# Cached attention and a gated MLP for one token: from groups of four heads with two K and two V buffers to groups of eight heads with three shared buffers

## The chip, the cores and the metric

The kernel runs on one core of a Trainium2 chip. Its work is done by five engines that run side by side and meet at semaphores: TensorE (PE; its weight loads are listed apart, as PEld), VectorE (DVE), ScalarE (ACT), GpSimd (POOL) and SyncE (SP), which issues nearly all transfers from HBM. PE multiplies what lies in SBUF and writes to PSUM. The metric is the device time of one execution in microseconds, lower is better; three executions of the kernel before were timed.

## What is computed

One token passes through an attention block with a long cache and then through a gated MLP, with a layer norm ahead of each and a residual after each. Everything is bf16; D = 640, 32 heads of 128, 4096 cached positions, MLP width 1728.

```
h = x + attention(layernorm(x)) @ wo
    q      = layernorm(x) @ wq                      # 32 heads x 128
    scores = q . k_cache * 128**-0.5                # 32 x 4096
    o      = softmax(scores) @ v_cache              # 32 x 128
h2 = h + (gelu(g) * u) @ w_down                     # g, u = layernorm(h) @ w_gate, w_up
```

K and V are 33.6 MB each, wq and wo 5.2 MB each, the three MLP matrices 2.2 MB each: 84.23 MB, each byte of which is used once.

## The kernel before, in words

`Sched` keeps a list of operations per engine, in the order in which the Python code calls them, and for each the semaphores it waits for. So the order of calls is the order of each engine's queue, and an engine whose first instruction waits holds back all behind it. SP's queue, which issues the loads, is such a queue too.

Heads are worked on in 8 groups of 4 (`HG`, `NG`). For a group, K is laid out with 32 partitions a head and 128 positions on each (`R`), 32 KB a partition, 4 MB in all; V likewise. There are two buffers for K and two for V, three product buffers `prod`, two score buffers `sc` and two probability buffers `P4`. The weights wq and wo share the `arena`; w_gate, w_up and w_down reuse K and V buffers when the last groups are done with them.

- Query (`query`, L318, L324): PE multiplies wq with x broadcast over 128 columns, five matmuls a group, and ACT copies each head's row onto its partitions in `qb`. It is done one group ahead.
- Scores, in four pieces of 32 positions: DVE multiplies K by q into `prod` (`mult`, L339), PE sums groups of 16 elements with an identity matrix (`fold`, eight matmuls, L359 and L350), and DVE sums the last 16 (`red`, L366).
- Softmax: a maximum on DVE, turned by PE (L378), a maximum over each head's partitions (L383), broadcast by PE (L388), and four exps on ACT, one per head, which write `P4` and the row sums (L395).
- Values (`values`, L406): matmuls with 16 columns of P as weights and 512 columns of V, all to the same 16 partitions of PSUM. `extract` (L421, L424) takes the useful blocks on DVE, `column` (L429) turns them. For the last group `values_last` (L414) uses V as weights.
- w_o (`project`, L612): the attention result is re-laid out (`spread`, `gather`, `place`) per pair of groups and multiplied with wo as weights, 160 matmuls of 32 columns, of which three quarters are issued ahead of the last group's values.
- Layer norm (L282 to L297), MLP (`up`, L659: 70 matmuls for gate and 70 for up, weights as the stationary side), gelu by an exp (L666 to L675), and the down projection (L697: 60 matmuls of 160 columns with one column of h as weights, to partitions 0, 32, 64 and 96). The last 64 rows of w_down come by eight small loads and a gathered vector (`rest`).

The loop over groups is written out as a software pipeline. In step n, DVE multiplies group n and finishes the maximum of group n-1, PE folds group n and between the folds runs the values of groups n-1 and n-2 in quarters. K(n+2) is issued once group n's products are made, V(n) once the values of group n-2 are done:

```python
        t_mul[3] = kfree[n] = mult(n, 3)
        if beside:
            values(p, 0, CH)
        fold(n, 3, t_mul[3])
...
            if n >= 2:
                load_v(n)
            if n + 2 < NG:
                load_k(n + 2)
```

Of the kernel before, what the change touches and what calls it, by code (L numbers as in the profile page):

```python
# [11 lines left out]
D = 640  # L12
H = 32
# [9 lines left out]
HG = 4  # L23
# [5 lines left out]
VR = 4  # L29
VM = VR * HG  # L30
NW = 4
HW = H // NW
DJ = 128 // HW
NFT = 13
NF = NFT + 1
WD_PARTS = (5, 4, 3, 1)

WD_COLS = []
for _n in WD_PARTS:
    _b = 128 * len(WD_COLS)  # L40
    WD_COLS += [(_b, _n, _i) for _i in range(_n)]
FREM = DF - NFT * 128
NRR = 2
NRP = FREM // NRR // 2
NRK = 32 + NRP
WIDE = 32
# [67 lines left out]
def bass_sequential_preLN__gqa_block_cached__glu_gated_geglu__decode_kernel(  # L114
# [16 lines left out]

    arena = sb("arena", [128, NC_D * H * DH], BF16)
    kbuf = [sb("kbuf%d" % i, [128, R, DH], BF16) for i in range(2)]
    vbuf = [sb("vbuf%d" % i, [128, R, DH], BF16) for i in range(2)]

    def over(name, base, shape):
        return nc.alloc_sbuf_tensor_at(name, shape, BF16, offset=nc.lookup_mloc(base).addr)

    wq_sb = over("wq_sb", arena, [128, NC_D, H * DH])
    wo_sb = over("wo_sb", arena, [128, NW, HW, D])
    wg_sb = over("wg_sb", kbuf[NG % 2], [128, NC_D, DF])
    wu_sb = over("wu_sb", kbuf[(NG + 1) % 2], [128, NC_D, DF])
    wd_sb = over("wd_sb", vbuf[NG % 2], [128, NFT + NRR, D])

    NPR = 3
    prod = [sb("prod%d" % i, [128, RP, DH], BF16) for i in range(NPR)]
    qb = sb("qb", [128, NG, DH], BF16)
    sc = [sb("sc%d" % i, [128, R], FP32) for i in range(2)]  # L150
    P4 = [sb("P4_%d" % i, [128, R, HG], BF16) for i in range(2)]
    RS = sb("RS", [128, H], FP32)
    mx = sb("mx", [128, NG], FP32)
    mrow = sb("mrow", [1, H], FP32)
    nb = sb("nb", [128, H], FP32)
    rz = sb("rz", [128, H], FP32)
    xm = sb("xm", [VM, VR, DH], FP32)
    xz = [sb("xz%d" % i, [VM, DH], FP32) for i in range(2)]
    rmask = sb("rmask", [VM, VR], FP32)
    hsel = sb("hsel", [VM, HG], FP32)  # L160
    aT = sb("aT", [128, H], BF16)
    aL = sb("aL", [128, HW, DJ], BF16)
    aP = sb("aP", [128, H], BF16)
    jmask = sb("jmask", [128, DJ], BF16)
    csel = sb("csel", [128, HW], BF16)
    jred = sb("jred", [128, DJ], FP32)
    cred = sb("cred", [128, HW], FP32)
# [8 lines left out]
    g_t = sb("g_t", [128, NF], FP32)  # L176
    t1 = sb("t1", [128, NF], FP32)
    t2 = sb("t2", [128, NF], FP32)
    t3 = sb("t3", [128, NF], FP32)
    e_t = sb("e_t", [128, NF], FP32)  # L180
    d_t = sb("d_t", [128, NF], FP32)
    r_t = sb("r_t", [128, NF], FP32)
    gu = sb("gu", [128, NF], FP32)
    hm = sb("hm", [128, NF], BF16)
    hq = sb("hq", [128, NRR], BF16)
    hr = sb("hr", [128, NRR], BF16)
    hcol = sb("hcol", [128, NRR], FP32)
    hrow = sb("hrow", [128, 128], BF16)
    o_sb = sb("o_sb", [128, D // 4], BF16)
    hx = sb("hx", [128, 32, NC_D], FP32)  # L190
    m32 = sb("m32", [128, 32], FP32)
    e4 = sb("e4", [128, 4], FP32)
# [3 lines left out]
    ones_bf = sb("ones_bf", [128, 128], BF16)  # L196
# [3 lines left out]
    pq = nc.alloc_psum_tensor("pq", [128, 512], FP32)  # L200
    pm = nc.alloc_psum_tensor("pm", [128, 512], FP32)
    po = nc.alloc_psum_tensor("po", [128, 512], FP32)
    pz = nc.alloc_psum_tensor("pz", [128, 512], FP32)
    pg = nc.alloc_psum_tensor("pg", [128, 512], FP32)
    pu = nc.alloc_psum_tensor("pu", [128, 512], FP32)
    pv = [pg, pu]


    t_one = S.op("vector", lambda v: v.memset(ones[:, :], 1.0))
    t_part = S.op("vector", lambda v: v.memset(part[:, :], 1.0 / D))  # L210
    S.op("vector", lambda v: v.memset(eps[:, :], EPS))
    t_onebf = S.op("vector", lambda v: v.memset(ones_bf[:, :], 1.0))
    t_p4 = [S.op("vector", lambda v, i=i: v.memset(P4[i][:, :, :], 0.0)) for i in range(2)]
    t_rs = S.op("vector", lambda v: v.memset(RS[:, :], 0.0))
# [3 lines left out]
    t_ibf = S.op("gpsimd", lambda g: g.affine_select(  # L218
        Ibf[:, :], ones_bf[:, :], pattern=[[1, 128]], compare_op=ALU.is_equal,
        fill=0.0, base=0, channel_multiplier=-1), [t_onebf])  # L220

    t_e4 = S.op("vector", lambda v: v.reduce_sum(
        e4[:, :], I32[:, :].rearrange("p (j i) -> p j i", j=4), axis=AX.X), [t_i32])
    hsum = hx[:, :, :].rearrange("p a b -> p (a b)")[:, 0:2 * NRP]
    t_hsum = S.op("vector", lambda v: v.reduce_sum(
        hsum, I32[:, 128 - FREM:128].rearrange("p (r i) -> p r i", i=NRR), axis=AX.X))
    t_hrow = S.op("vector", lambda v: v.memset(hrow[:, :], 0.0))
    t_hrow = S.op("vector", lambda v: v.tensor_copy(
        hrow[:, 0:64].rearrange("p (b r) -> p b r", b=2)[:, :, 0:NRP],
        hsum.rearrange("p (b r) -> p b r", b=2)), [t_hsum, t_hrow])  # L230
    t_hcol = S.op("vector", lambda v: v.reduce_sum(
        hcol[:, :], I32[:, 128 - FREM:128].rearrange("p (r i) -> p i r", i=NRR), axis=AX.X))
    t_m32 = S.op("vector", lambda v: v.reduce_sum(
        m32[:, :], I32[:, :].rearrange("p (j i) -> p i j", j=4), axis=AX.X))
    S.op("vector", lambda v: v.reduce_sum(
        rmask[:, :], I32[0:VM, 0:VM].rearrange("p (j h) -> p j h", h=HG), axis=AX.X))
    t_hsel = S.op("vector", lambda v: v.reduce_sum(
        hsel[:, :], I32[0:VM, 0:VM].rearrange("p (j h) -> p h j", h=HG), axis=AX.X))
    a = S.op("vector", lambda v: v.reduce_sum(
        jred[:, :], I32[:, :].rearrange("p (j c) -> p j c", c=HW), axis=AX.X))  # L240
    b = S.op("vector", lambda v: v.reduce_sum(
        cred[:, :], I32[:, :].rearrange("p (j c) -> p c j", c=HW), axis=AX.X))
    t_jm = S.op("vector", lambda v: v.tensor_copy(jmask[:, :], jred[:, :]), [a])
    t_cs = S.op("vector", lambda v: v.tensor_copy(csel[:, :], cred[:, :]), [b])


    d_wq = S.dma("sync", "wq", lambda s: s.dma_start(  # L247
        wq_sb[:, :, :], A_wq[:, :].rearrange("(p c) n -> p c n", c=NC_D)))

    def cache(src, g):  # L250
        return src[0, g * HG:(g + 1) * HG, :, :].rearrange("h (q r) d -> (h q) r d", r=R)

    d_k, d_v = [None] * NG, [None] * NG
    kfree, vfree = [None] * NG, [None] * NG

    def load_k(g):
        d_k[g] = S.dma("sync", "k%d" % (g % 2), lambda s: s.dma_start(
            kbuf[g % 2][:, :, :], cache(A_k_cache, g)), [kfree[g - 2] if g >= 2 else None])


    def load_v(g):
        d_v[g] = []
        cuts = [0, R]
        for i in range(len(cuts) - 1):
            lo, hi = cuts[i], cuts[i + 1]
            tok = S.dma("sync", "v%d_%d" % (g % 2, i), lambda s, lo=lo, hi=hi: s.dma_start(
                vbuf[g % 2][:, lo:hi, :], cache(A_v_cache, g)[:, lo:hi, :]),
                [vfree[g - 2] if g >= 2 else None])
            d_v[g] += [tok] * (hi - lo)


    load_k(0)
    load_k(1)
    load_v(0)


# [4 lines left out]
    def layernorm(src, t_src, o, dst, ps, beside=None):  # L281
        b = S.op("vector", lambda v: v.scalar_tensor_tensor(  # L282
# [4 lines left out]
        if beside is not None:  # L287
            beside()
        q = 2 * o
        d = S.op("vector", lambda v: v.scalar_tensor_tensor(  # L290
# [6 lines left out]
        return S.op("vector", lambda v: v.tensor_scalar(  # L297
# [3 lines left out]
    for c in range(NC_D):  # L301
        a = S.op("tensor", lambda t, c=c: t.matmul(
            pm[:, c:c + 1], x_sb[0:1, c::NC_D], ones_bf[0:1, 0:1],
            start=(c == 0), stop=(c == NC_D - 1), skip_group_check=True),
            [d_x, t_onebf], token=(c == NC_D - 1))
    t_x32 = S.op("vector", lambda v: v.tensor_copy(x32[:, :], pm[:, 0:NC_D]), [a])
    t_x32 = S.op("vector", lambda v: v.reduce_sum(st[:, 0:1], x32[:, :], axis=AX.X), [t_x32])
    t_xb = layernorm(x32, t_x32, 0, (
        xb[:, :, :], x32[:, :].unsqueeze(2).to_broadcast([128, NC_D, 128])), pz)


    t_qb = [None] * NG

    def query(g):
        tok = None
        for c in range(NC_D):
            n0 = g * HG * DH
            tok = S.op("tensor", lambda t, c=c, n0=n0: t.matmul(  # L318
                pq[:, :], xb[:, c, :], wq_sb[:, c, n0:n0 + HG * DH],
                start=(c == 0), stop=(c == NC_D - 1)),  # L320
                [t_xb, d_wq, t_qb[g - 1] if g else None], token=(c == NC_D - 1))
        for hh in range(HG):
            lo, hi = hh * PPH, (hh + 1) * PPH
            t_qb[g] = S.op("scalar", lambda a, lo=lo, hi=hi, hh=hh: a.copy(  # L324
                qb[lo:hi, g, :], pq[lo:hi, hh * DH:(hh + 1) * DH]), [tok])
        return tok


    fold_done, red_done = {}, {}
    t_exp, t_pv = [None] * NG, [None] * NG  # L330
    t_ext, t_acc = [None] * NG, [None] * NG
# [404 lines left out]
```

## Time and profile before

| | |
|---|---|
| device time, median of 3 | 203.99 us (203.86 to 205.19) |
| device time of the profiled execution | 203.82 us |
| its span in the profile | 202.6 us |
| granted TensorE clock, mean | 0.935 |
| bytes read from HBM | 84.23 MB, 416 GB/s over the span |

The span is the profiled part of an execution, from its first instruction to its last; the device time has 1.2 us more around it. The profile gives busy time by engine, 40 equal slices of the span, the transfer queues, the chain that ended last (followed back from the last instruction, at each step to what released it), and groups of instructions by line: their busy time in all, the mean length of one in ns, and the idle time of the engine just ahead of them with what ended it. Matmuls are pipelined, so a matmul's length is not the distance to the next; that distance is read from the timeline. Loads take these times from issue to landing, queueing included: K 25.1 us and V 23.2 us (medians), wq 15.3, w_gate 22.6, w_up 27.3.

### The profile page before, as it was taken

The numbers are of one execution on the slowest core, as the hardware profiler recorded it, in microseconds if no ns is written. First come the engines' busy times: TensorE is split into PE (matmuls) and PEld (weight loads), VectorE is DVE, ScalarE is ACT, GpSimd is POOL, SyncE is SP. The second block draws the span as 40 slices with busy tenths as digits, with TensorE's granted clock in tenths as the row PEclk, the third lists the DMA queues.
The fourth block names the chain that finished last, engine by engine and source line by source line (L and its number), as shares of the span: only waits on it lengthen the run. The fifth ranks groups of instructions, "written<-read, shape, count | busy, mean of one in ns | idle before, by whom it ended". The sixth has DMA issues, their size and how long they took to land.

```text
span 202.6 us, 2291 instructions
## 1 busy us (share of the span) xinstructions
PE 153.4 (76%) x1084; PEld 49.8 (25%) x860; DVE 116.1 (57%) x153; ACT 30.5 (15%) x110; POOL 2.4 (1%) x8
## 2 busy tenths in 40 slices
PE   1005348689969957999899399959777999977775
PEld 1001000002211220322122113212100244666572
DVE  6200087998199518883993499269999513301121
ACT  2002200006004200150060006000604004000000
POOL 1000000000000000000000000000000000200000
PEclk9999999999999996999999999999999999975555
DMA  7999999999999999999999999999999999989992
GB/s 251 412 469 414 414 434 453 459 414 414 421 450 427 459 409 414 440 429 440 443 421 414 434 440 440 434 427 411 440 427 446 385 427 457 450 382 438 423 396 102
DMA packets 3939, 84.37 MB, mean 416 GB/s; under 512 B 441, under 2 KB 570, under 8 KB 986
## 3 DMA queue, kind: packets, MB, share of 16 engines
q1 hardware_dynamic: 3928, 84.23, 97.4%
q8 instruction: 7, 0.11, 0.2%
q14 instruction: 2, 0.02, 0.0%
q10 hardware_dynamic: 2, 0.00, 0.0%
HBM read 84.23 MB, written 0.00 MB: 416 GB/s over the span
## 4 chain that ended last, share of the span: by engine, by line
DMA 60%; DVE 28%; PE 10%; issue 1%; SPq 0%; DVEq 0%
DMA kbuf<-in_A_k_cache_dram 47%; DVE prod L339 19%; DMA wu_sb<-in_B_w_up_dram 13%; DVE sc L366 4%; PE pu L406 4%; PE pf L350 3%; DVE xz L424 2%; PE pu L659 1%; DVE xm L421 1%; PE pf L697 1%; PE pf L359 1%; DVE mx L374 1%; DVE mrow L383 0%; SPq L247 0%; DVE o_sb L701 0%
## 5 line engine op out<-in xcount | busy, mean ns | idle before, releaser
L339 DVE TENSOR_TENSOR prod<-kbuf,qb 128x4096 bf16<-128x4096 bf16 x32 | 72.8, 2278 | 46.4 <-DMA kbuf<-in_A_k_cache_dram 46.4
L350 PE MATMUL pf<-prod,Ibf 128*128 128x512 bf16 x224 | 57.0, 397 | 0.0
L359 PE MATMUL pf<-prod,Ibf 128*128 128x512 bf16 x32 | 13.1, 410 | 24.9 <-DVE prod L339 24.9
L406 PE MATMUL pg<-vbuf,P 128*16 128x512 bf16 x128 | 29.9, 379 | 0.0
L366 DVE TENSOR_REDUCE sc<-pf 128x32 f32<-128x512 f32 x32 | 21.6, 676 | 4.2 <-PE pf L350 4.2
L406 PE MATMUL pu<-vbuf,P 128*16 128x512 bf16 x96 | 22.2, 379 | 0.0
L318 PE MATMUL pq<-wq_sb,xb 128*128 128x512 bf16 x40 | 12.1, 442 | 12.5 <-DMA wq_sb<-in_A_wq_dram 11.3
L391 ACT ACTIVATE nb<-pm 128x4 f32<-128x4 f32 x8 | 1.4, 173 | 118.6 <-PE pm L388 118.6
L395 ACT ACTIVATE P<-sc,nb 32x128 bf16<-32x128 f32 x32 | 18.5, 577 | 0.9
L406 PEld LDWEIGHTS pg<-vbuf,P 128*16 128x16 bf16 x128 | 10.6, 90 | 20.0 <-issue 5.2
L359 PEld LDWEIGHTS pf<-prod,Ibf 128*128 128x128 bf16 x32 | 3.2, 99 | 45.5 <-DVE prod L339 40.5
L406 PEld LDWEIGHTS pu<-vbuf,P 128*16 128x16 bf16 x96 | 8.1, 90 | 16.9 <-issue 6.9
L324 ACT CAST qb<-pq 32x128 bf16<-32x128 f32 x32 | 8.2, 256 | 16.0 <-PE pq L318 15.2
L318 PEld LDWEIGHTS pq<-wq_sb,xb 128*128 128x128 bf16 x40 | 3.8, 111 | 17.3 <-issue 13.0
L612 PE MATMUL pf<-aP,wo_sb 128*128 128x32 bf16 x160 | 7.1, 194 | 1.2 <-issue 1.0
L395 ACT ACTIVATION_READ_ACCUMULATOR P<-sc,nb 32x1 f32 x32 | 8.0, 250 | 0.0
L424 DVE TENSOR_REDUCE xz<-xm 16x128 f32<-16x512 f32 x7 | 7.3, 1040 | 0.2
L612 PEld LDWEIGHTS pf<-aP,wo_sb 128*128 128x128 bf16 x160 | 6.8, 131 | 1.9 <-issue 1.5
L388 PEld LDWEIGHTS pm<-mrow,ones 1*128 1x128 f32 x16 | 2.3, 183 | 12.6 <-issue 10.9
L414 PE MATMUL pq<-P,vbuf 128*128 128x32 bf16 x128 | 3.6, 188 | 1.4 <-DMA vbuf<-in_A_v_cache_dram 1.4
L421 DVE TENSOR_TENSOR xm<-pg,rmask 16x512 f32<-16x512 f32 x4 | 2.7, 672 | 3.4 <-PE pg L406 3.4
L429 PEld LDWEIGHTS po<-hsel,xz 16*128 16x128 f32 x14 | 2.0, 183 | 10.1 <-DVE xz L424 9.7
(85 smaller groups left out, 58.1 us busy)
## 6 DMA issues: line engine op xcount, KB each, us to landing
kbuf<-in_A_k_cache_dram SPq DMA_DIRECT2D x8, 4096.0 KB, 25.1
vbuf<-in_A_v_cache_dram SPq DMA_DIRECT2D x8, 4096.0 KB, 23.2
wq_sb<-in_A_wq_dram SPq DMA_DIRECT2D x1, 5120.0 KB, 15.3
wo_sb<-in_A_wo_dram SPq DMA_DIRECT2D x1, 3840.0 KB, 28.7
wg_sb<-in_B_w_gate_dram SPq DMA_DIRECT2D x1, 2160.0 KB, 22.6
wu_sb<-in_B_w_up_dram SPq DMA_DIRECT2D x1, 2160.0 KB, 27.3
wo_sb<-in_A_wo_dram SPq DMA_DIRECT2D x1, 1280.0 KB, 17.8
wd_sb<-in_B_w_down_dram SPq DMA_DIRECT2D x1, 800.0 KB, 16.0
```

Source lines behind the costliest of these rows:

```text
L318: tok = S.op("tensor", lambda t, c=c, n0=n0: t.matmul(pq[:, :], xb[:, c, :], wq_sb[:, c, n0:n0 + HG * DH], start=(c == 0), stop=(c == NC_D ...
L324: t_qb[g] = S.op("scalar", lambda a, lo=lo, hi=hi, hh=hh: a.copy(qb[lo:hi, g, :], pq[lo:hi, hh * DH:(hh + 1) * DH]), [tok])
L339: return S.op("vector", lambda v: v.tensor_tensor(out=prod[n % NPR][:, :, :], in0=kbuf[g % 2][:, s * RP:(s + 1) * RP, :], in1=qb[:, g, :]. ...
L350: return t.add_instruction(m)
L359: return t.matmul(dst, Ibf[:, :], src, start=True, stop=False)
L366: red_done[n] = S.op("vector", lambda v: v.reduce_sum(sc[g % 2][:, s * RP:(s + 1) * RP], pf[n % 2][:, :].rearrange("p (r w) -> p r w", r=R ...
L395: t_exp[g] = S.op("scalar", lambda a, lo=lo, hi=hi, h=h, hh=hh: a.activation(P4[g % 2][lo:hi, :, hh], sc[g % 2][lo:hi, :], ACTF.Exp, bias= ...
L406: t_pv[g] = S.op("tensor", lambda t, i=i, r=r, last=last: t.matmul(pv[g % 2][0:VM, :], P4[g % 2][:, r:r + VR, :], vbuf[g % 2][:, r:r + VR, :],
L414: t_pv[g] = S.op("tensor", lambda t, r=r: t.matmul(pq[:, 0:WIDE], vbuf[g % 2][:, r, :], P4[g % 2][:, r, :].unsqueeze(1).to_broadcast([128, ...
L421: a = S.op("vector", lambda v: v.tensor_tensor(out=xm[:, :, :], in0=pv[g % 2][0:VM, :].rearrange("p (r d) -> p r d", r=VR), in1=rmask[:, : ...
L424: t_ext[g] = S.op("vector", lambda v: v.reduce_sum(xz[g % 2][:, :], xm[:, :, :].rearrange("p r d -> p d r"), axis=AX.X), [a, t_acc[g - 2] ...
L612: tok = S.op("tensor", lambda t, c=c, cc=cc, first=first, last=last: t.matmul(pp[:, cc * WIDE:(cc + 1) * WIDE], wo_sb[:, w, c, cc::NC_D], ...
```

## The change

The new kernel works on 4 groups of 8 heads, with 16 partitions a head and 256 positions on each: a load of K or V is 64 KB a partition, 8 MB in all. There are three buffers `big`, shared by everything:

- `big[0]`: K0, V1, V2, then w_up and w_down
- `big[1]`: V0, K2, V3, then small tensors of the MLP
- `big[2]`: wq, K1, K3, then w_o and w_gate

Products are written over K in place. The query matmuls for two groups are made at once (20 matmuls to four PSUM banks), masked and summed on DVE. The softmax maximum is turned by a DVE transpose; one exp on ACT covers all 128 partitions; DVE spreads it over 8 columns with a mask to make P. The value matmuls have 32 columns of P as weights and write in turn to partitions 0, 32, 64 and 96. w_o, gate and up put the activations on the stationary side and the weights on the moving side, so their results are rows on partitions 0, 32, 64 and 96, which DVE transposes. The residual is added by four matmuls with x; the last 64 rows of w_down are one load and a 14th column. w_o is one load. The order of calls has the stages of a group one after another, but for the values of group 2, which follow the folds of group 3 on PE.

```diff
-HG = 4
+HG = 8
-    kbuf = [sb("kbuf%d" % i, [128, R, DH], BF16) for i in range(2)]
-    vbuf = [sb("vbuf%d" % i, [128, R, DH], BF16) for i in range(2)]
+    big = [sb("big%d" % i, [128, R, DH], BF16) for i in range(3)]
+    kb = [big[0], big[2], big[1], big[2]]
+    vb = [big[1], big[0], big[0], big[1]]
...
+        for c in range(NC_D):
+            for i in range(4):
+                n0 = g * HG * DH + 512 * i
...
+                tok = S.op("tensor", mm, [t_xb, d_wq, t_qt[0]], token=(c == NC_D - 1 and i == 3))
+        for i in range(4):
...
+                out=xm[lo:hi, :, :], in0=pq[i][lo:hi, :].rearrange("p (h d) -> p h d", d=DH),
+                in1=hmask[lo:hi, h0:h0 + 4].unsqueeze(2).to_broadcast([64, 4, DH]), op=ALU.mult),
...
     def mult(g, s):
-            out=prod[n % NPR][:, :, :], in0=kbuf[g % 2][:, s * RP:(s + 1) * RP, :],
+            out=kb[g][:, s * RP:(s + 1) * RP, :], in0=kb[g][:, s * RP:(s + 1) * RP, :],
...
+    def scores(g):
+        t_mul = mult(g, 0)
+        for s in range(NP):
+            fold(g, s, t_mul)
+            if s + 1 < NP:
+                t_mul = mult(g, s + 1)
+            red(g, s)
+        kfree[g] = fold_done[g * NP + NP - 1]
+
+    def soft(g):
+        a = vec(lambda v: v.reduce_max(mx[:, g:g + 1], sc[:, :], axis=AX.X), [red_done[g * NP + NP - 1]])
+        a = vec(lambda v: v.transpose(mt[:, :], mx[:, g:g + 1].to_broadcast([128, 32])), [a])
+        a = vec(lambda v: v.reduce_max(
+            mh[:, :], mt[:, :].rearrange("p (t i) -> p t i", t=2), axis=AX.X), [a])
...
+            ex[:, :], sc[:, :], ACTF.Exp, bias=nb[:, g:g + 1], scale=SCALE,
+            accum_out=rs[:, g:g + 1]), [a, t_p[g - 1] if g else None])
+        t_p[g] = vec(lambda v: v.tensor_tensor(
+            out=P[:, :, :], in0=ex[:, :].unsqueeze(2).to_broadcast([128, R, HG]),
+            in1=hmask_bf[:, :].unsqueeze(1).to_broadcast([128, R, HG]), op=ALU.mult),
...
+        t_z[g] = S.op("tensor", lambda t: t.matmul(
+            pz[:, 8:8 + HG], ones[:, :], rsm[:, :], start=True, stop=True), [a, t_rz[g - 1] if g else None])
+        t_rz[g] = vec(lambda v: v.reciprocal(rz[:, g * HG:(g + 1) * HG], pz[:, 8:8 + HG]), [t_z[g]])
+
+    def values(g):
+        for i in range(NV):
+            r, q = i * VR, 32 * (i % 4)
+            t_pv[g] = S.op("tensor", lambda t, i=i, r=r, q=q: t.matmul(
+                pv[g % 2][q:q + 32, :], P[:, r:r + VR, :], vb[g][:, r:r + VR, :],
+                start=(i < 4), stop=(i >= NV - 4)),
+                [t_p[g], d_v[g], t_qt[0], t_ext], token=(i == NV - 1))
+        vfree[g] = t_pv[g]
...
+    for g in range(0, NG, 2):
+        t_qlast = query(g)
+    load_k(1, t_qlast)
+    scores(0)
+    load_v(1, kfree[0])
+    soft(0)
+    values(0)
+    load_k(2, vfree[0])
+    outs(0)
+    scores(1)
+    load_k(3, kfree[1])
+    soft(1)
+    values(1)
+    load_v(2, vfree[1])
+    outs(1)
+    scores(2)
+    load_v(3, kfree[2])
+    soft(2)
+    scores(3)
+    values(2)
+    outs(2)
+    soft(3)
+    values(3)
+    t_aT = outs(3)
+
+    d_wo = S.dma("sync", "wo", lambda s: s.dma_start(
+        wo_sb[:, :, :], A_wo[:, :].rearrange("(p c) n -> p c n", c=QD)), [kfree[3]])
+    d_wg = load_w("wg", wg_sb, B_w_gate, kfree[3])
+    d_wu = load_w("wu", wu_sb, B_w_up, vfree[2])
...
+    for c in range(QD):
+        for j in range(4):
...
+                pd[32 * j:32 * j + 1, 0:NQ], aP[:, c:c + 1], wo_sb[:, c, j * NQ:(j + 1) * NQ],
...
+                b = S.op("tensor", lambda t, c=c, j=j, row=row, lhs=lhs: t.matmul(
+                    row[:, :, 0:NM], lhs,
+                    w[:, c, QF * j:QF * (j + 1)].rearrange("p (i b) -> p i b", b=NM),
...
+                if E0 <= 32 * j < E0 + EP:
+                    f0 = MF + 32 * j - E0
+                    S.op("tensor", lambda t, c=c, j=j, f0=f0, row=row, lhs=lhs: again(
```

`outs(g)` does for a group what `extract` and `column` did, on 128 partitions instead of 16, and then multiplies by the reciprocal `rz`.

## The prediction, made before the changed kernel was run

> **What bounds the kernel now.** I read the page from the top first: which engine is full, and whether the transfers ever stop.
>
> ```profile
> span 202.6 us, 2291 instructions
> PE 153.4 (76%) x1084; PEld 49.8 (25%) x860; DVE 116.1 (57%) x153; ACT 30.5 (15%) x110; POOL 2.4 (1%) x8
> DMA  7999999999999999999999999999999999989992
> q1 hardware_dynamic: 3928, 84.23, 97.4%
> ...
> DMA kbuf<-in_A_k_cache_dram 47%; DVE prod L339 19%; DMA wu_sb<-in_B_w_up_dram 13%; DVE sc L366 4%; PE pu L406 4%; PE pf L350 3%; DVE xz L424 2%; PE pu L659 1%; DVE xm L421 1%; PE pf L697 1%; PE pf L359 1%; DVE mx L374 1%; DVE mrow L383 0%; SPq L247 0%; DVE o_sb L701 0%
> ```
>
> No engine is full; the DMA row is, in every slice but the first and the last, and the queue is busy for 97.4% of the span. The chain alternates between waiting for K and multiplying it. So the kernel is one stream of 84.23 MB with the arithmetic beside it. The stretches from 30 to 150 us of the windows view carry 429, 439, 441, 425, 436, 422, 437 and 436 GB/s; weighted by length, 432. The wq wait on PE ends at 16.2, and the other 78.99 MB at 432 take 182.9 us: 199.1, where the last w_down load indeed ends a PE wait (199.8). Behind it lie 2.8 us of arithmetic and output. Second, the costs of the steps, from the groups, and PE's clock, from the timeline of PE:
>
> ```profile
> L339 DVE TENSOR_TENSOR prod<-kbuf,qb 128x4096 bf16<-128x4096 bf16 x32 | 72.8, 2278 | 46.4 <-DMA kbuf<-in_A_k_cache_dram 46.4
> L366 DVE TENSOR_REDUCE sc<-pf 128x32 f32<-128x512 f32 x32 | 21.6, 676 | 4.2 <-PE pf L350 4.2
> L395 ACT ACTIVATE P<-sc,nb 32x128 bf16<-32x128 f32 x32 | 18.5, 577 | 0.9
> L424 DVE TENSOR_REDUCE xz<-xm 16x128 f32<-16x512 f32 x7 | 7.3, 1040 | 0.2
> ```
> ```profile
> 70.23 3.62 PE L406 MATMUL pu<-vbuf,P 128*16 128x512 bf16 x16
> 77.31 0.61 PE L359 MATMUL pf<-prod,Ibf 128*128 128x512 bf16 x1 [3.46 <-DVE prod L339]
> 77.71 3.13 PE L350 MATMUL pf<-prod,Ibf 128*128 128x512 bf16 x7
> ...
> 86.28 0.38 PE L359 MATMUL pf<-prod,Ibf 128*128 128x512 bf16 x1
> 86.49 1.68 PE L350 MATMUL pf<-prod,Ibf 128*128 128x512 bf16 x7
> ...
> 197.94 0.84 PE L697 MATMUL pf<-wd_sb,hm 128*1 128x160 bf16 x20 [0.33 <-DVE hm L675]
> 198.71 0.18 PE L681 MATMUL pz<-hq,hrow 128*128 128x2 bf16 x1
> ```
>
> Columns: start, length, engine, line, idle time before. A fold of eight matmuls takes 1.9 us at full clock (86.28) and 3.5 after PE stood idle for 3.46 us (77.31; the windows view grants 0.50 there until 80.9). Sixteen value matmuls take 3.6 us, 0.22 each, one after another. At the end 20 matmuls of 160 columns start within 0.77 us, 0.0385 each, at a granted 0.50. At that clock a 512-column matmul takes 0.43 (wq, 5 in 2.29), so 160 columns take 0.133: the four output rows at partitions 0, 32, 64 and 96 run side by side, 3.5 deep.
>
> **The stream after.** The bytes are the same. K and V come in 8.39 MB, 19.4 us each at 432. If the queue never runs dry, landings are: K0 35.6, V0 55.0, K1 74.5, V1 93.9, K2 113.3, K3 132.7, V2 152.1, V3 171.5, w_o 183.7, gate 188.8, up 193.9, w_down 199.1. Larger pieces I price at nothing: the stream is already near 432 with 32 KB pieces, and wq with 40 KB shows no better rate. Each load waits for its buffer. The arithmetic below releases them at: V1 62, K2 74, K3 101, V2 113, V3 140, w_o and gate 170.6, up and w_down 174; the queue would run dry at 74, 94, 113, 133, 152 and 171, so only w_o (about 1.5 us of issue) leaves a gap, and nothing waits for it.
>
> **The arithmetic after.** What the change removes is the overlap: before, the value matmuls of group n-1 lie between the folds of group n; now scores, softmax, values and outputs of one group follow each other, and DVE's next multiplications stand behind that group's outputs in its queue.
>
> Queries: 20 matmuls each, 4.4 (full clock) to 8.6 us (half); I take 6.5, since the first 5 ran at half. DVE then makes four masked copies (0.65, from L421's rows of 512) and two sums (1.04): 4.7. From 16.2: 22.8; last copy 26.4, second query done 33.0, its DVE work 37.7. K0 is there at 35.6, so scores start at 37.7 (35.6 to 42).
>
> Scores of a group, eight pieces: DVE 2.20 + 0.60 from start to start, PE 1.9, so DVE sets it: 8 x 2.20 + 6 x 0.60 + the last fold 1.9 + last sum 0.7 = 23.9. PE is idle for over 3.5 us before each, so the first fold is cold, +1.4 as in the first group of before: 25.3. The lower end is 23.9; if all folds ran at half clock (3.5 a piece) it is 30.6. I take 25.3. In-place products cost nothing: same shape and types as L339.
>
> Softmax: maximum over 256 (0.29 for 128 plus 0.13) 0.4; transpose of 32 columns 0.2 (not in the trace; nearest 0.16 to 0.25); maximum and scaled sum 0.5; exp with its accumulator 0.8 (one of 128 takes 0.61 from start to start); P of 2048 elements with a repeated operand: aL, the same form, costs 0.29 for 128, 0.15 for 8, so 1.2 ns an element, 2.4 (at L339's rate 1.2). Row sums, their matmul and six hops: 0.8. Together 5.1 to the first value matmul; 3.9 to 5.9.
>
> Values: 64 matmuls of 512 columns, 32 wide, to four quadrants. One after another they cost 64 x 0.22 = 14; side by side like L697, 3.5 warm and 6.9 cold. L697 is the same form, so I take side by side. PE has then been idle for some 5 us: one cold window of 3.4 us, then warm, is 5.2 at the least; I take 6.0, and 3.6 where they follow folds.
>
> On this the Trainium skill, "TensorE: Matmul & The Clock Gate", Part 3, gives 2.38 for three column tiles of N=512, less than three. Scaled to four it would make the warm values 4.4 instead of 3.5 and the sum some 2 us longer. The trace's 3.5 of four, at half clock and 160 columns, is nearer this form, and decides here.
>
> Outputs of a group: 0.65 + 1.04 + a small f32 matmul 0.4 + 0.15 + hops: 2.4.
>
> A group is thus 25.3 + 5.1 + 6.0 + 2.4 = 38.8, just the 38.8 of its K and V. Scores start at 37.7, 76.5 (K1 74.5), 115.3 (K2 113.3). Those of group 2 end at 140.6, its softmax with the reciprocal at 146.0; scores of group 3 follow, to 171.3. Only then come values 2 (warm, behind the last fold at 170.6) 174.2, outputs 176.6, softmax 3 181.7, values 3 187.7, outputs 190.1. V3 landed at 171.5: it is no longer what is late.
>
> End: clears, aL, gather, copy 1.1 (191.2); w_o as 132 matmuls of 160 columns at 0.0385, 5.1 (196.3; before, three quarters were done under the last V load); row transpose 0.5 and layernorm 2.3 as before (199.1); gate, 20 of 416 columns at half clock, 0.35 for four, and 10 of 32: 2.1 (201.2; before 2.5); up 2.1 (203.3); transpose 0.6, product and hops 0.4 (204.3); down 56 x 0.0385 = 2.2 (206.5; the gathered remainder, 0.3, is gone); copy and output 2.1 as before: 208.6. Dropping the residual matmuls, the extra query copies on ACT and the eight small w_down loads saves nothing, since they were hidden under the stream.
>
> The span grows by 6.0. The profiled execution took 203.82 (0.17 under the median), so 209.8: 210.
>
> **Rivals.** (1) Not slower, the stream still hides it all. For it: the sum is only 6 us over, and 115.3 can fall to K2's landing at 113.3. Scores without cold folds (-2.8), softmax at 3.9 (-2.4) and values 3 warm (-2.5) bring the end under 201, and then w_down's landing at 199.1 sets it as before: 203.5. It decides once the path from K2 to the end is under 89 us; I have 93.3. Against: PE's idle gaps, which cost clock in this very trace.
> (2) The value matmuls don't overlap. 14.6 warm, 16.2 after idle: +10.2 a group three times, +11 for values 2, less waiting: near 250. For: L406 ran singly; against: those went to one quadrant, L697 to four.
> (3) Folds stay at half clock, 3.5 a piece against DVE's 2.8: scores 30.6, four times +5.3, values cold +3 in all, late V3: about 235. For: clock 0.50 from 180 on, with PE busy. Against: 1.00 between 30 and 60 us, where folds of 512 columns ran with gaps of 0.9 us.
> The Trainium skill's same page, Part 1, puts a PE that idled for a window of about 3.4 us at half clock until it was busy for one; the trace agrees (3.46 idle, 0.50 for 3.4).
>
> **How the numbers follow.** Forecast 0.62, rival 1 0.22, rival 2 0.08, rival 3 0.08. Own range of the forecast 204 to 219: the low end as in rival 1, the high end with queries +4.2, softmax +0.8 and values +0.9 in every group. The range 203.4 to 219 leaves out rivals 2 and 3 and a little below. About 1% (2.0 us) is what a measurement here can tell. Faster than 202 needs a stream faster than 432: 0.03. Within 1%: most of rival 1 and the low tail of the forecast: 0.25. Slower: 0.72.
>
> **What would show it.** Right: K loads never wait long on SP, DMA row full to about 199 minus a small gap near 171, then PE and DVE alone for 9 us; value matmuls start 0.055 to 0.11 apart; DVE the longest part of the chain. Wrong: value matmuls 0.2 apart; half clock inside the folds; P at 1.2 us; K3 or V3 issued after the queue ran dry.

## The result, and the profile after

| | before | after |
|---|---|---|
| device time, median of 22 runs each | 203.86 us (203.65 to 205.19) | 205.95 us (203.33 to 207.40) |
| ratio to before, with its 95% interval | | 1.0073 (1.0054 to 1.0092) |
| profiled execution | 203.82 us, span 202.6 | 207.06 us, span 205.8 |

The ratio leaves out runs more than 1.5% above the fastest of their kernel, so it is lower than the ratio of the medians, 1.010. The change costs 1 to 2 us, a third of what was forecast. Twelve further runs gave 205.62 (203.74 to 207.24), 1.0071 (1.0038 to 1.0103). The profiled execution of the changed kernel lies 1.1 us above its median; that matters below. The new thing in the times is their spread: 4 us, where all but four runs of before lie within 0.6.

From the page of the changed kernel: span, busy time, the clock and transfer rows, and the chain.

```profile
span 205.8 us, 1609 instructions
PE 117.2 (57%) x826; PEld 24.6 (12%) x552; DVE 130.1 (63%) x162; ACT 6.0 (3%) x18; POOL 1.1 (1%) x6
PEclk9999969669998596999958889999589999757555
DMA  7999999999999999999999999999999989999960
q1 hardware_dynamic: 2392, 84.23, 95.5%
...
DVE 55%; PE 33%; DMA 8%; issue 2%; ACT 2%; DVEq 0%
```

The queue is still nearly full, but the chain has changed hands: DVE and PE hold 88% of it, and the 8% of DMA is wq, ahead of everything. In the table of waits only two loads are waited for at all, by PE and its weight loads, both at the start:

```profile
PE pq L299 <- DMA wq_sb<-in_A_wq_dram: 12.0, 1, 12.0
PEld po L269 <- DMA x_sb<-in_A_x_dram: 2.5, 1, 2.5
```

So in this execution the stream no longer sets the end, from wq on. It has one gap, where w_o waits for the last fold of K3. From the windows view (stretch, its length, busy time and count by engine, clock, DMA share, GB/s):

```profile
169.00:170.00 1.00, 1.00 (x21) 0.54 (x24) 0.69 (x1) 0.00 (x0) 0.00 (x0) 1.00 0.01 0
170.00:171.00 1.00, 1.00 (x28) 0.48 (x20) 0.00 (x0) 0.00 (x0) 0.00 (x0) 1.00 1.80 508
```

The share of 1.80 in the second row shows that a packet is booked whole where it starts (the first loads, from 1.5 to 2.0 us, have 3.74); so the first row says that none started for about a microsecond, not that nothing was moved. The gap is at most that long. The chain in order of time (start, length, what), pieces of group 0 and of group 3:

```profile
61.47 1.52 PE pf L285 x7
63.01 0.70 DVE sc L341
...
65.50 2.29 DVE P L366
...
68.58 5.35 PE pq L379 x63
73.95 0.70 DVE xm L387
...
76.34 2.21 DVE big L322
...
78.99 2.94 PE pf L285 x7
...
114.03 2.21 DVE big L322
...
169.06 3.60 PE pq L379 x64
...
179.82 6.04 PE pq L379 x55
...
189.15 4.46 PE pf L465 x117
```

The reader is to see one stage behind the other, with nothing beside it: the last fold of group 0 ends at 63.0, its values start at 68.6, DVE starts on group 1 at 76.3. And the same 64 value matmuls take 3.60 us at 169.06, right behind folds, and 6.04 at 179.82, after PE has been idle. The groups:

```profile
L322 DVE TENSOR_TENSOR big<-big,qb 128x4096 bf16<-128x4096 bf16 x32 | 72.7, 2281 | 0.0
L379 PE MATMUL pq<-big,P 128*32 128x512 bf16 x256 | 20.4, 489 | 0.0
L366 DVE TENSOR_TENSOR P<-ex,hmask_bf 128x2048 bf16<-128x2048 bf16 x4 | 9.2, 2293 | 2.7 <-ACT ex L363 2.7
```

In-place products take 2281 ns against 2278 before. The 256 value matmuls keep PE busy for 20.4 us in all, against 52.1 for the 224 of the first seven groups of before. P costs 2.29 us, 1.12 ns for each of its 2048 elements on a partition, near the 1.2 ns of the forecast.

### The profile page after: what moved, and what is told of

It reads as the page before. It is cut to its first block, busy times and chain, and to the rows that moved or that the text cites. A ratio compares the mean times of both kernels' runs of the same rounds, so it can differ in the third digit from the quotient of the medians.

```text
span 205.8 us, 1609 instructions
## 1 busy us (share of the span) xinstructions
PE 117.2 (57%) x826; PEld 24.6 (12%) x552; DVE 130.1 (63%) x162; ACT 6.0 (3%) x18; POOL 1.1 (1%) x6
## 4 chain that ended last, share of the span: by engine, by line
DVE 55%; PE 33%; DMA 8%; issue 2%; ACT 2%; DVEq 0%
DVE big L322 30%; PE pq L379 10%; PE pf L285 9%; DVE sc L341 8%; DMA wq_sb<-in_A_wq_dram 8%; PE pq L285 5%; DVE P L366 4%; PE pf L465 2%; DVE xm L306 2%; DVE xz L390 2%; PE pf L334 2%; PE pq L299 2%; DVE xz L311 1%; DVE xm L387 1%; ACT ex L363 1%
## 5 line engine op out<-in xcount | busy, mean ns | idle before, releaser
L322 DVE TENSOR_TENSOR big<-big,qb 128x4096 bf16<-128x4096 bf16 x32 | 72.7, 2281 | 0.0
L285 PE MATMUL pf<-big,Ibf 128*128 128x512 bf16 x224 | 60.0, 413 | 0.0
L334 PE MATMUL pf<-big,Ibf 128*128 128x512 bf16 x32 | 13.9, 434 | 36.6 <-DVE big L322 36.6
L379 PE MATMUL pq<-big,P 128*32 128x512 bf16 x256 | 20.4, 489 | 0.0
L306 DVE TENSOR_TENSOR xm<-pq,hmask 64x512 f32<-64x512 f32 x8 | 5.5, 688 | 22.3 <-PE pq L285 22.1
L299 PE MATMUL pq<-wq_sb,xb 128*128 128x512 bf16 x10 | 5.0, 502 | 16.0 <-DMA wq_sb<-in_A_wq_dram 12.0
L285 PE MATMUL pq<-wq_sb,xb 128*128 128x512 bf16 x30 | 11.2, 494 | 0.0
L366 DVE TENSOR_TENSOR P<-ex,hmask_bf 128x2048 bf16<-128x2048 bf16 x4 | 9.2, 2293 | 2.7 <-ACT ex L363 2.7
L379 PEld LDWEIGHTS pq<-big,P 128*32 128x32 bf16 x256 | 7.7, 120 | 12.4 <-issue 9.3
L465 PE MATMUL pf<-wo_sb,aP 128*1 128x160 bf16 x128 | 4.4, 338 | 0.1
L311 DVE TENSOR_REDUCE xz<-xm 128x128 f32<-128x512 f32 x4 | 4.1, 1022 | 0.1
L390 DVE TENSOR_REDUCE xz<-xm 128x128 f32<-128x512 f32 x4 | 4.1, 1018 | 0.1
L465 PEld LDWEIGHTS pf<-wo_sb,aP 128*1 128x1 bf16 x128 | 4.1, 124 | 0.3 <-DVE aP L455 0.3
## 6 DMA issues: line engine op xcount, KB each, us to landing
wq_sb<-in_A_wq_dram SPq DMA_DIRECT2D x1, 5120.0 KB, 15.4
wu_sb<-in_B_w_up_dram SPq DMA_DIRECT2D x1, 2160.0 KB, 23.8
```

Of the source, the lines that this page charges most:

```text
L285: return t.add_instruction(m)
L299: return t.matmul(dst, xb[:, c, :], src, start=(c == 0), stop=last)
L306: a = t_qt[0] = vec(lambda v, i=i, lo=lo, hi=hi, h0=h0: v.tensor_tensor(out=xm[lo:hi, :, :], in0=pq[i][lo:hi, :].rearrange("p (h d) -> p h ...
L311: t_qf[0] = vec(lambda v: v.reduce_sum(xz[:, :], xm[:, :, :].rearrange("p h d -> p d h"), axis=AX.X), [a, t_qb[gg - 1] if gg else None])
L322: return vec(lambda v: v.tensor_tensor(out=kb[g][:, s * RP:(s + 1) * RP, :], in0=kb[g][:, s * RP:(s + 1) * RP, :], in1=qb[:, g, :].unsquee ...
L334: return t.matmul(dst, Ibf[:, :], src, start=True, stop=False)
```

## The experiments

Theory: arithmetic sets the end of the changed kernel; PE's half clock after each idle stretch is part of it and makes the times spread; the stream's own end lies only 2 to 3 us below. Rivals: the stream with its gap sets the end; or the clock matters little; and, for one term of the sum, that the four quadrants of the value matmuls don't run side by side.

### One quadrant

```diff
-            r, q = i * VR, 32 * (i % 4)
+            r, q = i * VR, 0
-                start=(i < 4), stop=(i >= NV - 4)),
+                start=(i == 0), stop=(i == NV - 1)),
```

(`outs` reads partitions 0 to 31 alone.)

> All 64 value matmuls of a group write to partitions 0 to 31 instead of to four quadrants in turn; the outputs of a group are taken from those 32 partitions. Theory (four quadrants run side by side: 3.6 us warm, 5.3 to 6.0 after an idle stretch in the changed kernel's profile): in one quadrant they run one after another, 0.22 us apart warm and 0.43 in the first cold window, 14 to 17 us a group, all of it on the path: about +10 us in each of four groups, 246 us. Rival (the quadrants bring little; the matmuls were held by something else): under 215 us.

Measured: 242.67 us, one run, against 203.98 for before beside it. From PE's timeline of this kernel, the values of group 0:

```profile
67.27 15.40 PE L379 MATMUL pq<-big,P 128*32 128x512 bf16 x64
```

15.4 us instead of 5.4 (and 14.0, 0.22 each, for group 2, behind folds), and the time is 3 us under the 246 expected. The quadrants are worth some 37 us; without them this change would have been a bad one. The forecast of side-by-side columns, read from 20 small matmuls of the kernel before, holds for 32 columns and 512 as well.

### Half of w_o, in both kernels

```diff
-        wo_sb[:, :, :], A_wo[:, :].rearrange("(p c) n -> p c n", c=QD)), [kfree[3]])
+        wo_sb[:, 0:QD // 2, :], A_wo[:, :].rearrange("(p c) n -> p c n", c=QD)[:, 0:QD // 2, :]), [kfree[3]])
-                pd[32 * j:32 * j + 1, 0:NQ], aP[:, c:c + 1], wo_sb[:, c, j * NQ:(j + 1) * NQ],
+                pd[32 * j:32 * j + 1, 0:NQ], aP[:, c:c + 1], wo_sb[:, c % (QD // 2), j * NQ:(j + 1) * NQ],
```

In the kernel before, the same with `0:HW // 2` in its two loads of w_o and `c % (HW // 2)` in `project`.

> The changed kernel loads only half of w_o (2.62 MB less, 6.1 us of stream at 432 GB/s) and uses that half twice, so that the matmuls stay as many and as long. Theory (arithmetic sets the end): 205.4 to 206.2, no change. Rival (the stream sets the end): 3 to 6 us lower, 200 to 203.

> The same cut in the kernel before: half of w_o loaded, used twice. Theory (that kernel is set by the stream): lower by up to 6.1 us, until its own arithmetic sets the end: 197.8 to 200.5. Rival (its arithmetic is as late as its stream): 202.5 to 204.

Measured: after 205.24 (203.04 to 207.04, 10 runs), before 201.71 (200.47 to 202.65, 4 runs; ratio 0.987, 0.980 to 0.994). In the changed kernel the median falls by 0.4 to 0.7, just below the 205.4 to 206.2 expected, and the ratio to before is 1.0000 (0.9955 to 1.0045) instead of 1.0073, which is 1.5 us. Four of its ten runs lie at 203.0 to 203.2, where only one of the 34 uncut runs lies under 203.5; the other six, at 204.9 to 207.0, lie where uncut ones do. The windows view of one of those six (206.30 us):

```profile
187.00:196.00 9.00, 4.88 (x137) 4.24 (x137) 3.28 (x14) 0.47 (x2) 0.00 (x0) 0.81 0.75 307
196.00:202.00 6.00, 4.18 (x72) 2.20 (x56) 2.81 (x10) 0.22 (x1) 0.00 (x0) 0.72 0.01 4
```

From 196 on almost nothing is moved (4 GB/s), and that execution still has a span of 205.0. So in the longer executions the stream is not what holds the changed kernel's end. In the shortest ones it seems to be; the profile of the early kernel below, at 203.97 us, shows such an end. Of the kernel before the theory was too generous: it fell by 2.3 us (1.2 to 4.0 by the interval) and not by 3.5 to 6, so it was bound by the stream, but its own arithmetic lies only some 2.3 us below. In the chain of that kernel no load stands behind the K that landed at 133.7.

### Unread matmuls that keep PE warm

```diff
+    def keep(n, ps):
+        for _ in range(n):
+            S.op("tensor", lambda t: t.matmul(
+                ps[:, :], Ibf[:, :], xb[:, 0:4, :], start=True, stop=True), [t_ibf, t_xb], token=False)
...
+    keep(26, pf[1])
+    query(0)
+    keep(14, pf[1])
+    t_qlast = query(2)
+    keep(26, pf[1])
...
+        keep(20 if g < 3 else 17, pg)
         t_z[g] = S.op("tensor", lambda t: t.matmul(
...
+        keep(6, pg)
         t_acc[g] = S.op("tensor", lambda t: t.matmul(
...
+    keep(9, pg)
     scores(1)
```

(`keep(9, pg)` stands ahead of `scores(2)` and `scores(3)` too.)

> The changed kernel with matmuls whose result nobody reads (a 128x128 identity times 512 columns of the broadcast x, into a free PSUM bank) put on PE where it stands idle: ahead of the queries, between and behind them, during each softmax and around each output step. Theory (arithmetic sets the end, and PE's half clock after each idle stretch is the part of it that varies): queries 2.4 and 2 us shorter, first folds 1.4 shorter four times, values 1.7 to 2.5 shorter in groups 0, 1 and 3, then the stream's end at about 199 to 200 of the span takes over: 203.3 us, 202.6 to 204.0. Rival 1 (the clock is not what costs): 205.9 or a little more. Rival 2 (the stream with its gap ahead of w_o already sets the end): no more than 0.5 lower.

Measured: 203.09 us (202.82 to 204.07, and one run of 285.62, which no trace here explains), ratio to before 0.9955 (0.9932 to 0.9977). 2.9 us under the changed kernel, from nothing but extra work on PE. Two parts of it tell where:

```diff
-        keep(20 if g < 3 else 17, pg)
+        keep(20 if g < 2 else 0, pg)
```
```diff
-        keep(20 if g < 3 else 17, pg)
+        keep(0 if g < 2 else 20 if g < 3 else 17, pg)
```

The first is the early kernel (queries, groups 0 and 1), the second the late one (from ahead of the scores of group 2 on); `keep(6, pg)`, `keep(9, pg)` and the three at the queries are divided likewise.

> The unread matmuls only up to the outputs of group 1 (queries, groups 0 and 1). Theory (arithmetic sets the end, but groups 1 and 2 can't start before K1 at 74.1 and K2 at 113.1 have landed): the 6 to 8 us saved early shrink to what group 2 starts earlier, 114.0 to 113.1, so 0.9 us: 205.0, 204.5 to 205.5. Rival (each microsecond of clock won anywhere counts): 203.1, as with all of them.

> The unread matmuls only from ahead of the scores of group 2 on. Theory: first folds of groups 2 and 3 are 1.4 us shorter each and the last values 2.4, 5.2 us off the path, of which the stream's end leaves some 2.8: 203.1, 202.7 to 203.9. Rival (the clock counts early, where most idle time is): above 205.

Measured: early 206.00 (203.97 to 206.99, 5 runs; 1.0131, 1.0107 to 1.0154), late 203.01 (202.91 to 203.14, 4 runs; 0.9956, 0.9941 to 0.9972). The early one brings nothing that five runs show (0.9 was expected, and lies within its spread of 3.0). Its chain shows why. DVE stands ready and waits for K2 until 113.5, where without the extra matmuls it had been busy until 114.0:

```profile
69.16 44.30 DMA big<-in_A_k_cache_dram
113.47 2.30 DVE big L327
```

That profiled execution is the shortest of the five, 203.97 us, and its end is the stream's again. From PE's timeline, part of the down projection:

```profile
199.87 0.70 PE L529 MATMUL pf<-wd_sb,hm 128*1 128x160 bf16 x16 [0.77 <-DMA wd_sb<-in_B_w_down_dram]
```

The late one has the whole gain. From PE's timeline of the late kernel, the values of groups 2 and 3:

```profile
165.46 3.64 PE L385 MATMUL pq<-big,P 128*32 128x512 bf16 x64
...
176.02 3.64 PE L385 MATMUL pq<-big,P 128*32 128x512 bf16 x64
```

3.64 for the last values instead of 6.08, after a start 3.7 us earlier. Its windows view grants 1.00 from 173 to 180 us, where the changed kernel had 0.85, and 0.79 against 0.66 from 180 to 187. And its chain has gone back to the stream:

```profile
165.53 3.60 PE pq L385 x64
169.13 0.02 issue
169.15 24.91 DMA wu_sb<-in_B_w_up_dram
194.05 0.04 issue
194.10 0.59 PE pq L492 x5
```

So the late version and the full one beat the kernel before too, each by 0.9 to 1.0 us against the runs of that kernel beside it (204.01 and 203.98).

### Another order at the end

```diff
-    outs(2)
     soft(3)
     values(3)
+    outs(2)
```

> One change of order only: softmax and values of group 3 are called ahead of the outputs of group 2, so that DVE makes P for group 3 beside the values of group 2, and the outputs of group 2 beside the values of group 3. Theory (arithmetic sets the end): values of group 3 start about 4 us earlier (175.7 instead of 179.8) and PE, idle for less than 3.4 us before, may stay warm; the stream's end then leaves 2 to 2.8 us of it: 203.2 to 204.0. Rival (the stream's end with its gap ahead of w_o already sets the time): 205.5 or more.

> All unread matmuls and the order of swap. Theory (with a warm PE the stream sets the end): no change against the warm kernel's 203.1, 202.7 to 203.4, though the arithmetic is some 3 us shorter. Rival (arithmetic still sets it there): 200 to 202.

Measured: swap 204.60 (203.78 to 205.24, 10 runs; 1.0022, 1.0001 to 1.0042), warm_swap 203.37 (202.95 to 204.54, 12 runs; 0.9973, 0.9953 to 0.9993). The swap gains 1.4 us where 2 to 2.8 were expected: the values of group 3 did start 4.4 us earlier, but PE did not stay warm, and they took longer than ever:

```profile
168.64 3.60 PE pq L379 x64
172.33 2.29 DVE P L366
174.82 0.60 PE pm L372 x2
175.42 6.43 PE pq L379 x64
```

PE is idle from 172.2 to 174.8, 2.6 us. The windows view of this kernel (the clock is the third number from the end) shows the rest:

```profile
174.00:175.00 1.00, 0.18 (x1) 0.18 (x2) 0.77 (x2) 0.00 (x0) 0.00 (x0) 0.69 0.67 287
175.00:176.00 1.00, 1.00 (x10) 0.62 (x14) 0.55 (x2) 0.00 (x0) 0.00 (x0) 0.50 1.06 451
...
180.00:182.00 2.00, 2.00 (x26) 0.79 (x18) 0.00 (x0) 0.00 (x0) 0.00 (x0) 0.70 0.85 369
```

The clock fell at about 174.4 (0.69 is a mean of 1.00 and 0.50) and came back at about 181.2, 6.8 us later, so nearly all of the values ran at half. The expectation that an idle stretch under 3.4 us leaves PE warm is wrong. On top of warm PE the swap brings nothing, as expected of a kernel that waits for its stream.

### The stream under the warm kernel

The late kernel again, with half of w_o as above; and the changed kernel unaltered beside it.

> The kernel with the unread matmuls from group 2 on, and half of w_o loaded (used twice, as in the other halved kernels). Theory (once PE is warm, the stream sets the end: its profile waits for w_o 1.1 us, for w_up and for the last w_down piece): now lower than its 203.0, by about the 2 us that were waited, 200.5 to 202.0. Rival (203 is the arithmetic of this order): 202.6 to 203.4.

> The changed kernel unaltered, beside the kernels of this call, for the spread of its times: 203.3 to 207.4 so far, half of them within 205.4 and 206.5. Theory (where PE's clock window falls against the idle stretches differs from run to run, and the stream does not absorb it): the spread stays 3 us or more, that of the kernel with unread matmuls under 0.6. Rival (the spread is the chip's or the stream's): both alike.

Measured: 197.49 us (196.74 to 198.28, 4 runs; 0.9676, 0.9655 to 0.9697), 5.5 us lower than with all of w_o. That is outside the 200.5 to 202 expected. The late kernel's profile names waits of 1.1 us for w_o and 1.8 for w_up, 2.9 in all; the rest lies in the clock behind them. The w_o matmuls and the down projection, from PE's timeline of the late kernel:

```profile
183.92 4.03 PE L474 MATMUL pf<-wo_sb,aP 128*1 128x160 bf16 x128 [1.07 <-DMA wo_sb<-in_A_wo_dram]
197.45 2.15 PE L527 MATMUL pf<-wd_sb,hm 128*1 128x160 bf16 x56 [1.05 <-DVE hm L521]
```

and from the chain with half of w_o:

```profile
183.63 2.41 PE pf L474 x128
193.84 1.17 PE pf L527 x56
```

The same matmuls are 1.6 and 1.0 us shorter. The granted clock from 184 to 188 us is 1.00 there, against 0.57 with all of w_o, and in the down projection 1.00 against 0.50. With the 2.9 us of waits that makes the 5.5. That PE fell to half clock because it stood waiting is likely, but not shown: in the profile of the full version the w_o matmuls took 2.4 us behind a like wait of 1.1. The same cut brought 0.4 to 0.7 by the medians, and 1.5 by the ratios, with a PE that runs cold, and from 110 us on no load stands in the chain of the late kernel with half of w_o. So the theory's two halves are shown: with warm PE the stream sets the end; with cold PE arithmetic does, but for the shortest executions. The unaltered kernel again spread over 3.5 us; the kernels with unread matmuls over 0.2 (late), 1.3 (all, but for the one run), 1.6 (with the swap), 1.5 (late, with half of w_o) and 3.0 (early), so the expected 0.6 held for one of five.

## Why the prediction was right and wrong

The direction held, and so did the mechanism in most executions; the size did not: the forecast was +6.0 us, the medians differ by 2.1, and the rival "the stream still hides it all" would have said 203.5. The truth lay between: the forecast's mechanism in the longer executions, the rival's in the shortest. By its steps, against the profiled execution:

| step | forecast | measured |
|---|---|---|
| scores start | 37.7 | 38.2 |
| scores of a group | 25.3 | 25.2 to 25.5 |
| softmax, to the first value | 5.1 | 4.8 to 4.9 |
| values, after idle (groups 0, 1, 3) | 6.0 | 5.4, 5.2, 6.1 |
| values, behind folds (group 2) | 3.6 | 3.6 |
| outputs of a group | 2.4 | 2.4 |
| scores of group 2, of group 3 start | 115.3, 146.0 | 114.0, 144.4 |
| outputs of group 3 done | 190.1 | 188.3 |
| w_o, 132 matmuls | 5.1 | 4.5 |
| gate starts | 199.1 | 196.2 |
| down projection starts, ends | 204.3, 206.5 | 201.7, 203.8 |
| span | 208.6 | 205.8 |

The order of events, the buffers' release times (63.0, 74.0, 100.8, 111.6, 138.7, 169.1 by SP's timeline) and the gap ahead of w_o came out as written. The side-by-side columns, the 2.4 us for P and the cold folds, each read from rows of the kernel before, came out too.

What failed is the size of three terms of the sum. The steps were "one cold window of 3.4 us, then warm, is 5.2 at the least; I take 6.0", "w_o as 132 matmuls of 160 columns at 0.0385, 5.1", and the softmax, "Together 5.1 to the first value matmul". Values measured 0.6 and 0.8 less in groups 0 and 1 (not in group 3), w_o 0.6 less, each softmax 0.2 to 0.3 less. None is large, and the scores started 0.5 later; together they make most of the 2.8 us by which the span is shorter than the forecast. All three were taken too high, so their errors did not cancel.

The term for w_o had a second fault. Its rate was read off a burst of 20 matmuls at half clock. In this profile w_o did run at half clock (0.50 in each microsecond from 189 to 194) and took 4.4 us for 128 matmuls, 0.0347 each. At full clock, as in the profile of the early kernel, the same 128 took 2.4. So the term had some 2 us of play downwards, which neither the range nor the first rival counts.

The remaining 1.1 us is the profiled execution against the median. The forecast was a single sum with fixed cold penalties. The clock's half stretches differ from run to run. In three profiles of this order (207.06, 206.56 and, with half of w_o, 206.30 us) the last values took 6.1, 5.8 and 6.4 us and the w_o matmuls 4.4, 4.4 and 3.7; in one of 203.97 us (early kernel, the same code from group 2 on) they took 5.1 and 2.4. Unread matmuls remove the time, so that the clock costs it is shown. That the clock makes all of the spread is likely, but not shown: the spread was small, 0.2 us, only in the late kernel, where the stream covers what varies, and 1.5 in the same kernel with half of w_o.

The first rival's point of decision was right: "once the path from K2 to the end is under 89 us". The 93.3 beside it counts to the end of the span. Measured in the same way, from the start of group 2's scores, it is 91.8 in the profiled execution (205.8 less 114.0), 2.8 above. In the early kernel's 203.97 us it is 89.1, and there PE waits for the last w_down piece as the rival says. That should have moved chance: with every early term capped by K2's landing at 113, the forecast had 4 us of margin, and the terms behind K2 had more play than that. The early kernel shows the cap, the late one what lies behind it. Two slips in the working don't change the result: the terms of the scores add up to 23.8 and not 23.9, and the half clock near 77 us of the profile before ended at 80.7 by its windows, not 80.9.

The second rival (value matmuls one after another) is out: 242.7 us is its price, where I had written "near 250". The third (folds at half clock throughout) is out too: only the first folds of a group were cold. The Trainium skill, "TensorE: Matmul & The Clock Gate", Part 3, gives a speedup of 2.38 for three column tiles; scaled to four, an estimate, that makes the warm values 4.4 us. Four tiles took 3.6, against 64 x 0.22 one after another, close to a full factor of four.

## What to carry to other kernels

A kernel that a transfer stream covers can lose most of its overlap and pay little, as long as the serial path stays under the stream; so work out the slack (here some 2.3 us before the change, about zero or below after it) ahead of any single term. Where PE waits for another engine in bursts, its price is the wait plus the half clock behind it (here 2.4 us on the last values and about 2 on w_o), and matmuls that nobody reads can be cheaper than the clock they keep, if they stand where the path is not capped by a load. When many terms are chosen between bounds, see what the sum does if all err the same way.

## What the runs showed of the hardware that was not expected

Four 32-column value matmuls on four quadrants take 3.64 us for 64 of 512 columns, 0.057 us each, at full clock; in one quadrant 64 took 15.4 us including the start at half clock. The clock's record in the trace of the changed kernel holds stretches at 0.50 of 3.41 or 6.83 us only, until the last one, and changes on one grid of 3.41 us; an idle stretch of 2.6 us was enough to halve it (swap), while gaps of 0.9 us within the folds did nothing. The Trainium skill, "TensorE: Matmul & The Clock Gate", Part 1, calls the window free-running, and the one grid agrees with that; its figure of one idle window, about 3.4 us, was not needed in full, as the 2.6 us show. Removing 2.62 MB of stream was worth 5.5 us to a kernel whose profile named 2.9 us of waits of PE for loads behind wq; the matmuls behind those waits, at half clock for the most part, make up the rest.
